# Moving the attention steps of batches 1 and 2 to other places in batch 0 of an attention and bilinear-layer kernel

## The chip, the cores and the metric

The kernel runs on one NeuronCore of a Trainium2 chip. A core has five engines that each work through their own instruction list in order: TensorE (PE; its weight loads are shown as PEld), VectorE (DVE), ScalarE (ACT), GpSimd (POOL, unused here) and SyncE (SP, which issues most of the DMAs). [...] The metric is the device time of one execution in microseconds (us). The kernel before the change took 482.41 us (median of three runs, 482.38 to 482.61).

## The reference

Attention between 512 tokens and 32 states in each of 8 batches and 8 heads, in both directions, then a bilinear layer with two more matrix products:

```python
def _attn_ref(x, state):                       # x (8, 8, 512, 64), state (8, 8, 32, 64)
    scores = scale * np.matmul(x, state.transpose(0, 1, 3, 2))
    a = softmax(scores)                        # over the 32 states
    xread = np.matmul(a, state)
    scores2 = scale * np.matmul(state, x.transpose(0, 1, 3, 2))
    a2 = softmax(scores2)                      # over the 512 tokens
    sread = np.matmul(a2, x)
    return np.concatenate([xread, sread], axis=2)

def _moe_ref(x, w1, w2, w3, w_out):            # x: 8 * 544 rows of 512; w1, w2 (512, 1024)
    a = x @ w1
    b = x @ w2
    h = a * b @ w3
    return (h @ w_out).astype(np.float32)
```

## The kernel before

**The algebra.** Since `xread` is `a @ state`, the kernel multiplies the states by the weights first (`sw`, "state times weights") and the softmax by the result afterwards. `w3 @ w_out` is formed once (`w34`). The softmax over states, transposed, is `at`; the one over tokens is `a2`. Operands of the large products are split into two float32r parts, `hi` and `lo`, by a cast on ACT and a subtraction on DVE (`split`, L100 to L104), and each product is the sum of three.

**The prologue.** The weights arrive as the bits of float64 numbers. `to_f32` (L107) makes float32 of a chunk of 128x1024: ACT turns the high words into a float (`w_sb<-raw` or `w<-raw`, L123) and takes the low words' share (`ulps<-raw`, L131; on DVE, L127, for the first chunks), and after a `yield` DVE shifts (L135) and adds (L139). `raw` has three buffers and `ulps` two. Eight chunks of w1 and w2 go to eight places of `w_sb`: chunks 0 to 3 serve columns 0 to 511 of both (`convert_half(0..3)`), chunks 4 to 7 the other half. `w34` (L629) makes rows of the product in fp32. In the prologue ACT and DVE run in the order in which the code is written, the `go(...)` calls; PE and SP do so in the whole program (`manual_schedule`). Behind `order.close()` the framework's scheduler sets the order on ACT and DVE, by priorities and the `issue_after` hints.

**Batch 0.** `stage1` (L357) is called for eight blocks `ft` of 128 hidden columns: 24 products into a tile of two PSUM banks, then `hidden`: ACT copies one bank (L326), DVE multiplies by the other (L327), `split` makes `g_hi` and `g_lo`. `stage2` and `early_stage2` (L371) project them in pieces of 12 products. Between them stand the small products: a **unit** (`sw_steps`, eight instructions at L152 on 64x32 sub-arrays, recorded as 16) makes one tile of `sw`, the **scores** of a batch are such a unit too, and the **read** (L268, 32 instructions recorded as 64, on 128x32 sub-arrays) makes `sread`. A row of them between products on the full 128x128 array is called a block here. Scores, units, `stage1` sums and reads take their PSUM tile in turn from a pool of three two-bank tiles (`two_banks()`, `ps`): each waits until the engine that reads the third one back has done so.

**Batches 1 to 7** (`quarter_batch`) make the 512x512 product from seven quarter products; the combinations of `w34` for them are made in batch 0 by `combine_weights(k)`, k = 0 to 3 (DVE L413 to L420, an ACT cast, a DVE subtraction; all four go through one buffer `g_x`). Each batch's read and units and the scores of the batch after next form one block.

**A batch's attention steps** (`attention_steps`): the generator `scores` makes the scores, two softmaxes (DVE L200 to L244, ACT L213 and L224), transposes both (`token_order` L229, then 16 small DMAs on SP's queue, `move_blocks` L177; `at` L249) and splits `at`. The `yield`s let the caller spread it. `read_state` multiplies a2 by the tokens (`x_s`, one buffer), scales the result on DVE (`scaled`, L273) and frees its PSUM tile by that.

Of the kernel before, what the change touches and what calls it, by code (L numbers as in the profile page):

```python
# [29 lines left out]
P = 128  # L30
NF = 512
NW = 1024
# [7 lines left out]
def attn_bilinear_kernel(  # L40
# [66 lines left out]
    def to_f32(pool, src, out, ends=(NW,), loads=(), wout=None):  # L107

        raw = pool.tile([P, NW], mybir.dt.int64, name="raw", bufs=3)
        ulps = pool.tile([P, NW], I32, name="ulps", bufs=2)
        parts = [slice(*ends) for ends in zip((0, *ends), ends)]
        for start, stop in zip((0, *loads), (*loads, NW)):
            nc.sync.dma_start(out=raw[:, start:stop], in_=src[:, start:stop])
        for part in parts:  # L120
            words = raw[:, part].bitcast(I32).rearrange("p (n k) -> p k n", k=2)
            high, low = words[:, 1], words[:, 0]
            nc.scalar.activation(  # L123
                out=out[:, part], in_=high.bitcast(F32), func=AF.Prelu, scale=2.0**-112, alpha=-(2.0**32)
            )
            if len(parts) > 1:
                nc.vector.tensor_scalar(  # L127
                    out=ulps[:, part], in0=low.bitcast(U32), scalar1=2.0**-29, scalar2=None, op0=ALU.mult
                )
            else:  # L130
                nc.scalar.activation(out=ulps[:, part], in_=low.bitcast(U32), func=AF.Copy, scale=2.0**-29)  # L131
        yield
        for part in parts:
            bits = out[:, part].bitcast(I32)
            nc.vector.tensor_scalar(out=bits, in0=bits, scalar1=3, scalar2=None, op0=ALU.logical_shift_left)  # L135
            for dest, start, stop in ((wout, 0, DO), (out, DO, NW)) if wout is not None else ((out, 0, NW),):
                piece = slice(max(start, part.start), min(stop, part.stop))
                if piece.start < piece.stop:
                    nc.vector.tensor_tensor(  # L139
                        out=dest[:, piece].bitcast(I32), in0=out[:, piece].bitcast(I32), in1=ulps[:, piece], op=ALU.add  # L140
                    )
# [30 lines left out]

    def move_blocks(dest, src):
# [7 lines left out]
    def attention_steps(b):  # L181
# [3 lines left out]
        def scores():  # L185
# [10 lines left out]
            s1 = work_tile()  # L196
# [8 lines left out]
            nc.vector.transpose(out=flat(s1), in_=flat(ps))  # L205
            if b <= PLAIN:
                token_maxima()
# [19 lines left out]
            def token_order():  # L227
                blocks = work_tile()
                nc.vector.transpose(out=flat(blocks), in_=flat(e2))  # L229
                a2["t"] = work_tile() if b < PLAIN else att.tile([P, KT, S], F32, name="e2", bufs=1)  # L230
# [4 lines left out]
            if b > PLAIN:  # L235
                token_order()
                yield
# [5 lines left out]
            nc.vector.reciprocal(out=sum1, in_=sum1)  # L243
            nc.vector.tensor_tensor(  # L244
# [5 lines left out]
            if b > PLAIN:  # L250
                yield
            at_tiles[b] = [att.tile([P, KT, S], F32R, name=f"at_{part}", bufs=1) for part in ("hi", "lo")]
            last = split(*at_tiles[b], at)
            if b <= PLAIN:
                yield
                with tc.issue_after(last[1].ins):
                    token_order()
# [60 lines left out]
    last_split, stored, last_unit = [], [], []  # L318
# [4 lines left out]
    def hidden(ps, n, g_hi, g_lo):  # L323
        a_sb = main.tile([P, NF], F32, name="tmp", bufs=4)
        with tc.high_priority():
            nc.scalar.copy(out=a_sb[:, :n], in_=ps[:, 0, :n])  # L326
            nc.vector.tensor_tensor(out=a_sb[:, :n], in0=a_sb[:, :n], in1=ps[:, 1, :n], op=ALU.mult)  # L327
# [60 lines left out]
    reads = {}  # L388

    def side_steps():  # L390

        scores, reads[1], _ = attention_steps(1)
        w = sw_steps(1)
        softmax = scores()

        def rest():

            with tc.issue_after(stored[0].ins):
# [73 lines left out]
    def quarter_batch(b):  # L472
# [33 lines left out]
        def next_scores(b):  # L506

            if b < B:
                scores, reads[b], _ = attention_steps(b)
                softmaxes[b] = scores()  # L510
                next(softmaxes[b])

        raw = whole_tile(main, F32)
        stage1_pair(b, 0, raw)
        if b == PLAIN:
            next_scores(b + 1)
            load_x(b + 2)
            first_moves = reads[b](own_banks)
            next(first_moves)
            next(softmaxes[b + 1])  # L520
        softmax = softmaxes.get(b + 1, iter(()))
        next(softmax, None)
        if b == PLAIN:
            next(first_moves, None)
# [5 lines left out]
        if b > PLAIN:  # L530
            next(softmax, None)
# [9 lines left out]
        if b == PLAIN:  # L541
            with behind(took):
                next(softmax)
# [89 lines left out]
    def convert_half(n):  # L633

        return to_f32(pro, w12[n], places[n])
# [38 lines left out]
    go(w2_0), go(w3_6), go(softmax), go(w3_6)  # L674
    w34(5)
    go(softmax)
    go(w2_0)
# [3 lines left out]
    load_tokens(0)  # L681
# [5 lines left out]
    w34(7, range(LAST, FT))  # L687
    finish(7)
    order.close()
    for quarter in range(QT):  # L690
        stage1(0, 2 * quarter, gs)
        if quarter == 1:
            run(sw_steps(0)[2:])
        if quarter:
            early_stage2(quarter - 1)
        if quarter == 1:
            side = side_steps()
        elif quarter == 2:
            run(side.pop(0))
# [124 lines left out]
    softmaxes = {}  # L824
# [48 lines left out]
```

## Time and profile before

| | us |
|---|---|
| median of the runs | 482.41 |
| the profiled execution | 482.62 |
| its span, first to last instruction | 480.8 |
| PE busy | 473.8 |
| DVE busy | 407.7 |
| ACT busy | 239.5 |

The profiled execution's time holds 1.8 us around the span. A row of the timeline gives the start (us from the span's start), how long the merged instructions took, the engine, the line, the operation, the tiles written and read, their shape and count, and in brackets how long the engine had been idle and what ended it. A matmul's row shows its modelled end, so rows of PE overlap: what matters is the distance between starts. A row of the windows gives each engine's busy time in a stretch, the granted TensorE clock and the DMA engines' share.

### The profile page before, as it was taken

What the parts mean: (1) busy time and instruction counts of PE and PEld (TensorE: products, weight loads), DVE (VectorE), ACT (ScalarE), POOL (GpSimd) and SP (SyncE); (2) the same over time, 40 slices, a digit from 0 to 9 for tenths busy, and PEclk for the clock granted to TensorE, in tenths of its full rate; (3) what the DMA queues carried; (4) which work ended last, traced back from release to release, by engine and by line L of the source; (5) the groups of instructions that cost most, each with busy time, mean ns of one, the idle gap of its engine ahead of it and who ended that gap; (6) DMA issues with size and microseconds to landing.
All of it is one profiled execution on the core that took longest, in us unless ns stands there. A gap on an engine that the chain in (4) does not pass through costs nothing.

```text
span 480.8 us, 7935 instructions
## 1 busy us (share of the span) xinstructions
PE 473.8 (99%) x3174; PEld 358.1 (74%) x3174; DVE 407.7 (85%) x511; ACT 239.5 (50%) x306; POOL 0.2 (0%) x4
## 2 busy tenths in 40 slices
PE   7999999999999999999999999999999999999996
PEld 5444457777788688878877887888688868888885
DVE  5669898899789997999699969987998796569987
ACT  4777785464444633643463446254624470335652
POOL 0000000000000000000000000000000000000000
PEclk9999999999999999999999999999999999999999
DMA  8996891432531522052215112421321102001101
GB/s 339 365 365 252 341 354 27 116 110 67 193 77 34 181 70 42 25 207 60 35 46 191 49 30 87 157 57 25 110 70 25 19 26 75 1 0 45 45 1 44
DMA packets 55716, 52.42 MB, mean 109 GB/s; under 512 B 41856, under 2 KB 50560, under 8 KB 51072
## 3 DMA queue, kind: packets, MB, share of 16 engines
q1 hardware_dynamic: 46752, 43.34, 27.7%
q10 hardware_dynamic: 8928, 8.59, 5.1%
q8 instruction: 25, 0.41, 0.4%
q14 instruction: 11, 0.09, 0.1%
HBM read 38.27 MB, written 8.91 MB: 98 GB/s over the span
## 4 chain that ended last, share of the span: by engine, by line
PE 86%; DVE 5%; DMA 5%; ACT 2%; issue 1%; SPq 0%; DVEq 0%; ACTq 0%
PE ps L439 32%; PE ps L466 16%; PE ps_a L466 12%; PE ps L152 6%; PE ps_o L371 5%; PE ps L357 5%; DMA raw<-in_w_k_dram 3%; PE ps L754 3%; PE ps_o L629 3%; PE ps L755 2%; DMA raw<-in_w3t_dram 2%; PE ps L268 2%; PE ps_a L152 1%; DVE tmp L450 1%; ACT ulps L131 1%
## 5 line engine op out<-in xcount | busy, mean ns | idle before, releaser
L439 PE MATMUL ps<-at_lo,sw_hi 128*128 128x512 f32 x224 | 87.4, 390 | 0.0
L439 PE MATMUL ps<-at_hi,sw_hi 128*128 128x512 f32 x224 | 87.3, 390 | 0.0
L439 PE MATMUL ps<-at_hi,sw_lo 128*128 128x512 f32 x224 | 87.3, 390 | 0.0
L102 ACT CAST g_hi<-g_x 128x1024 fp32r<-128x1024 f32 (+2 forms) x61 | 56.7, 939 | 55.2 <-DVE g_x L447 42.3
L103 DVE TENSOR_TENSOR g_lo<-g_x,g_hi 128x1024 fp32r<-128x1024 f32 (+2 forms) x61 | 65.3, 1080 | 9.5 <-ACT g_hi L102 9.4
L445 ACT COPY g_x<-ps 128x1024 f32<-128x1024 f32 x28 | 28.3, 1012 | 73.1 <-PE ps L439 45.2
L447 DVE TENSOR_TENSOR g_x<-g_x,ps 128x1024 f32<-128x1024 f32 x28 | 34.0, 1215 | 29.2 <-PE ps L439 29.2
L439 PEld LDWEIGHTS ps<-at_hi,sw_lo 128*128 128x128 f32 x224 | 42.1, 188 | 8.8
L439 PEld LDWEIGHTS ps<-at_lo,sw_hi 128*128 128x128 f32 x224 | 42.1, 188 | 8.7
L439 PEld LDWEIGHTS ps<-at_hi,sw_hi 128*128 128x128 f32 x224 | 42.1, 188 | 8.4
L466 PE MATMUL ps<-t,g_hi 128*128 128x512 f32 x180 | 45.3, 393 | 0.0
L450 DVE TENSOR_TENSOR g_x<-g_x 128x1024 f32<-128x1024 f32 (+1 forms) x32 | 36.9, 1154 | 0.4
L466 PEld LDWEIGHTS ps<-t,g_hi 128*128 128x128 f32 x180 | 32.3, 189 | 5.6
L450 DVE TENSOR_TENSOR tmp<-tmp,ps 128x512 f32<-128x512 f32 (+1 forms) x48 | 31.3, 651 | 2.0
L103 DVE TENSOR_TENSOR sw_lo<-ps,sw_hi 128x1024 fp32r<-128x1024 f32 (+1 forms) x28 | 30.6, 1138 | 0.2 <-ACT sw_hi L102 0.2
L466 PE MATMUL ps_a<-wo,g_hi 128*128 128x512 f32 x120 | 29.8, 390 | 0.0
L629 PE MATMUL ps_o<-w_sb,w 128*128 128x512 f32 x64 | 28.5, 599 | 0.5 <-DVE w L139 0.5
L466 PEld LDWEIGHTS ps_a<-wo,g_hi 128*128 128x128 f32 x120 | 22.5, 188 | 4.6
L466 PE MATMUL ps<-t,g_lo 128*128 128x256 f32 x180 | 25.6, 284 | 0.0
L102 ACT CAST sw_hi<-ps 128x1024 fp32r<-128x1024 f32 (+1 forms) x28 | 25.2, 973 | 0.6 <-PE ps L152 0.5
L152 PE MATMUL ps<-w_sb,st 64*32 64x512 f32 (+1 forms) x448 | 24.7, 561 | 0.0
L123 ACT ACTIVATE w_sb<-raw 128x1024 f32<-128x1024 f32 (+3 forms) x18 | 18.8, 1057 | 11.8 <-DMA raw<-in_w_k_dram 9.6
(116 smaller groups left out, 776.4 us busy)
## 6 DMA issues: line engine op xcount, KB each, us to landing
raw<-in_w_k_dram SPq DMA_DIRECT2D x8, 1024.0 KB, 6.9
x_d<-in_x_d_dram SPq DMA_DIRECT2D x8, 1024.0 KB, 5.2
raw<-in_w_dram SPq DMA_DIRECT2D x8, 1024.0 KB, 6.9
x_s<-in_x_s_dram SPq DMA_DIRECT2D x8, 1024.0 KB, 5.2
out_dram<-tmp ACTq DMA_DIRECT2D x56, 128.0 KB, 1.8
raw<-in_w3t_dram SPq DMA_DIRECT2D x4, 1024.0 KB, 7.6
e<-work SPq DMA_DIRECT2D x112, 32.0 KB, 1.9
out_dram<-tmp ACTq DMA_DIRECT2D x4, 256.0 KB, 2.0
```

The costliest lines, as they stand in the source:

```text
L102: nc.scalar.copy(out=hi, in_=src),
L103: nc.vector.tensor_tensor(out=lo, in0=src, in1=hi.bitcast(F32), op=ALU.subtract),
L123: nc.scalar.activation(out=out[:, part], in_=high.bitcast(F32), func=AF.Prelu, scale=2.0**-112, alpha=-(2.0**32))
L152: nc.tensor.matmul(ps[j * NS:(j + 1) * NS, q], sts[b][rows, j], moving(rows, j), start=True, stop=True)
L357: nc.tensor.matmul(ps[:, i], w[:, kt, c:c + P], a[:, kt], start=(k == 0), stop=(k == 3 * KT - 1))
L371: nc.tensor.matmul(by_halves(ps[:, :DO]), g, wo[w][:, ft], start=(ft == 0 and k == 0), stop=(ft == FT - 1 and k == 2))
L439: nc.tensor.matmul(ps[:, kk], w[:, kt, cols], a[:, kt], start=(k == 0), stop=(k == 3 * KT - 1))
L445: nc.scalar.copy(out=mine, in_=ps)
L447: return nc.vector.tensor_tensor(out=mine, in0=mine, in1=ps, op=ALU.mult)
L450: return nc.vector.tensor_tensor(out=out, in0=x, in1=y, op=op)
L466: nc.tensor.matmul(ps[:, tt, 1] if n else ps[:, tt], part, weights[:, 0] if n else weights, start=(fresh and k == 0 and n == parts[0]), st ...
L629: nc.tensor.matmul(w34_ps[i][:, :DO], w3s[i][:, k * P:(k + 1) * P], w_out[k], start=(k == 0), stop=(k == FT - 1))
```

## The change

The steps are the same; several are called elsewhere:

- `w3_6`'s second half (shift and add on DVE) is called one step of the softmax earlier: `scores` has one more `yield` ahead of the multiplication by the reciprocal (batch 0 only), and the calls in the prologue follow.
- Chunk 4 of w1/w2 is loaded into the tokens' buffer `x_s` in the prologue (`load_half(QT)`), where the tokens of batch 0 were loaded; those come behind `load_x(1)` now. Chunk 7's low words are taken on DVE instead of ACT.
- `token_order` of batch 0 (a transposition on DVE, then 16 DMAs) is called in the prologue, by way of the yields.
- The scores of batch 1 are called right behind units 2 and 3 of batch 0, in one block with them. Their transposed copy lies in `sread`, which is not yet written then. `token_order` of batch 1 comes ahead of the sums.
- The read of batch 1 and the scores of batch 2 join units 2 and 3 of batch 1; they were called in `quarter_batch(1)` behind its first pair of sums.
- `combine_weights(0)` is started a quarter later, and its two steps hang on other instructions.

```diff
-    def to_f32(pool, src, out, ends=(NW,), loads=(), wout=None):
+    def to_f32(pool, src, out, ends=(NW,), loads=(), wout=None, raw=None, on_vector=False):
-        raw = pool.tile([P, NW], mybir.dt.int64, name="raw", bufs=3)
+        if raw is None:
+            raw = pool.tile([P, NW], mybir.dt.int64, name="raw", bufs=3)
+            for start, stop in zip((0, *loads), (*loads, NW)):
+                nc.sync.dma_start(out=raw[:, start:stop], in_=src[:, start:stop])
...
-            if len(parts) > 1:
+            if len(parts) > 1 or on_vector:
                 nc.vector.tensor_scalar(
                     out=ulps[:, part], in0=low.bitcast(U32), scalar1=2.0**-29, scalar2=None, op0=ALU.mult
                 )
...
-            s1 = work_tile()
+            s1 = as_work(sread) if b == PLAIN else work_tile()
...
             yield
-            if b > PLAIN:
-                token_order()
+            if b >= PLAIN:
+                yield from token_order()
                 yield
...
+            if b < PLAIN:
+                yield
             nc.vector.tensor_tensor(
                 out=s1v, in0=s1v, in1=sum1.unsqueeze(2).broadcast_to([P, J, NS]), op=ALU.mult
             )
...
+        def second_read():
+            second = reads[1]()
+            next(second)
+            run(w[2:])
+            next_scores(2)
+            load_x(3)
+            yield from second
+
         first_read = reads[0]()
-        moves = lambda: first_read
         return [
-            [partial(islice, softmax, 3), partial(load_x, 2)], [partial(islice, first_read, 1), w[0], w[1]], [], [rest, moves],
-            [w[2], w[3]], [],
+            [partial(islice, first_read, 1), w[0], w[1]],
+            [], [rest, lambda: first_read], [second_read], [lambda: islice(softmaxes[2], 1)],
         ]
...
     def convert_half(n):
-        return to_f32(pro, w12[n], places[n])
+        return to_f32(pro, w12[n], places[n], raw=halves_ahead.get(n), on_vector=n == 2 * QT - 1)
+    def load_half(n):
+        place = att.tile([P, NT, H, D], F32, name="x_s", bufs=1)
+        halves_ahead[n] = place.rearrange("p t h d -> p (t h d)").bitcast(mybir.dt.int64)
+        nc.sync.dma_start(out=halves_ahead[n], in_=w12[n])
...
-    go(w2_0), go(w3_6), go(softmax), go(w3_6)
+    go(w2_0), go(w3_6), go(softmax), go(w3_6), go(softmax)
     w34(5)
-    go(softmax)
-    go(w2_0)
+    go(softmax), go(w2_0), go(softmax)
...
-    load_tokens(0)
+    load_half(QT)
...
         if quarter == 1:
             run(sw_steps(0)[2:])
+            next_scores(1)
+            load_x(2)
+            side = side_steps()
...
         if quarter == 0:
             run([partial(convert_half, n) for n in range(4, 2 * QT)])
             load_x(1)
-            with tc.issue_after(last_split[1].ins):
-                go(softmax)
+            load_tokens(0)
+            go(softmax)
...
-        elif quarter == 1:
-            first_sums = combine_weights(0)
-            with tc.issue_after(last_unit[1].ins):
-                go(first_sums)
+        elif quarter < 3:
+            with tc.issue_after(last_mult[0].ins):
+                go(softmaxes[1])
+            if quarter == 2:
+                first_sums = combine_weights(0)
+        else:
             with tc.issue_after(last_split[1].ins):
                 go(first_sums)
```

What this does to the engines' lists, at the three places of which the prediction speaks:

**ACT, the conversion of chunks 4 to 7, before.** `sw_hi` are the casts of the first units, `wo` that of `w34`; the two passes of a chunk are `ulps` and `w_sb`.

```order
L102 CAST sw_hi<-ps_346 128x2x256
L102 CAST sw_hi<-ps_359 128x2x256
L102 CAST wo<-ps_o 128x2x256
L131 ACTIVATE ulps<-raw 128x1024
L123 ACTIVATE w_sb<-raw 128x1024 x2
```

The same place after the change:

```order
L102 CAST sw_hi<-ps_346 128x2x256
L132 ACTIVATE ulps<-x_s 128x1024
L102 CAST sw_hi<-ps_359 128x2x256
L102 CAST wo<-ps_o 128x2x256
L132 ACTIVATE ulps<-raw 128x1024
L124 ACTIVATE w_sb<-x_s 128x1024
L124 ACTIVATE w_sb<-raw 128x1024
```

Chunk 4 is read from `x_s`, and chunk 5's `ulps` pass stands ahead of chunk 4's `w_sb` pass.

**DVE, from chunk 6 to the first three multiplications of `hidden` (L327, in the change L337), before.** The three read the PSUM tiles of the first three `stage1` sums: 406, 426 and 500.

```order
L103 TENSOR_TENSOR wo<-ps_o,wo 128x2x256
L135 TENSOR_SCALAR w_sb<-w_sb 128x1024
L139 ISA w_sb<-w_sb,ulps 128x2048
L327 TENSOR_TENSOR tmp<-tmp,ps_406 128x512
L327 TENSOR_TENSOR tmp<-tmp,ps_426 128x512
L103 TENSOR_TENSOR g_lo<-tmp,g_hi 128x512 x2
L229 STREAM_TRANSPOSE work<-e_261 128x1024
L327 TENSOR_TENSOR tmp<-tmp,ps_500 128x512
```

After the change, where the same sums lie in 408, 428 and 500:

```order
L103 TENSOR_TENSOR wo<-ps_o,wo 128x2x256
L136 TENSOR_SCALAR w_sb<-w_sb 128x1024
L128 TENSOR_SCALAR ulps<-raw 128x1024
L140 ISA w_sb<-w_sb,ulps 128x2048
L337 TENSOR_TENSOR tmp<-tmp,ps_408 128x512
L136 TENSOR_SCALAR w_sb<-w_sb 128x1024
L140 ISA w_sb<-w_sb,ulps 128x2048
L337 TENSOR_TENSOR tmp<-tmp,ps_428 128x512
L103 TENSOR_TENSOR g_lo<-tmp,g_hi 128x512 x2
L337 TENSOR_TENSOR tmp<-tmp,ps_500 128x512
```

Chunk 6 now stands ahead of the first multiplication and chunk 7 between the first and the second; one `ulps` pass is new on DVE; the transposition of `e` went ahead of all rows shown.

**PE, the block of units 2 and 3 of batch 1, after the change** (before, its rows 2 and 3 alone stood here):

```order
L277 MATMUL ps_866<-x_s,e_637 32x64 x32
L153 MATMUL ps_904<-w_sb,st 32x512 x8
L153 MATMUL ps_917<-w_sb,st 32x512 x8
L153 MATMUL ps_930<-x_d,st 32x512 x8
L382 MATMUL ps_o<-wo,g_hi 128x512 x2
```

The scores of batch 2 (930) are the third tile behind the read (866) and take its PSUM tile, which `scaled` frees. On DVE these rows lead up to it:

```order
L103 TENSOR_TENSOR sw_lo<-ps_787,sw_hi 128x1024
L103 TENSOR_TENSOR t<-g_x,t 128x4x256
L437 TENSOR_TENSOR g_x<-wo 128x4x256
L442 TENSOR_TENSOR g_x<-g_x 128x2x256
L103 TENSOR_TENSOR at_lo<-work,at_hi 128x1024
L443 TENSOR_TENSOR g_x<-g_x 128x256
L444 TENSOR_TENSOR g_x<-g_x 128x256
L103 TENSOR_TENSOR t<-g_x,t 128x4x256
L437 TENSOR_TENSOR g_x<-wo 128x4x256
L282 TENSOR_TENSOR scaled<-ps_866,sum_596 128x128
```

All of combination 1 (the first row `g_x<-wo` to the second `t<-g_x,t`) and the first addition of combination 2 stand ahead of `scaled`.

More of the change, by code (lines that the diff above doesn't have):

```diff
@@ L243, in scores @@
             nc.vector.reciprocal(out=sum1, in_=sum1)
+            if b < PLAIN:
+                yield
             nc.vector.tensor_tensor(
@@ L249, in scores @@
             nc.vector.transpose(out=flat(at), in_=flat(s1))
-            if b > PLAIN:
+            if b != PLAIN:
                 yield
             at_tiles[b] = [att.tile([P, KT, S], F32R, name=f"at_{part}", bufs=1) for part in ("hi", "lo")]
-            last = split(*at_tiles[b], at)
-            if b <= PLAIN:
+            split(*at_tiles[b], at)
+            if b < PLAIN:
                 yield
-                with tc.issue_after(last[1].ins):
-                    token_order()
+                yield from token_order()
         def read_state(place=two_banks):
@@ L386, in store, with next_scores @@
             queue.dma_start(out=dest, in_=o[first:first + n])
-    reads = {}
+    reads, softmaxes = {}, {}
+    def next_scores(b):
+        if b < B:
+            scores, reads[b], _ = attention_steps(b)
+            softmaxes[b] = scores()
+            next(softmaxes[b])
     def side_steps():
-        scores, reads[1], _ = attention_steps(1)
         w = sw_steps(1)
-        softmax = scores()
+        softmax = softmaxes[1]
         def rest():
-            with tc.issue_after(stored[0].ins):
+            with tc.issue_after(stored[0].ins), tc.issue_after(last_mult[0].ins):
                 yield from softmax
+        def second_read():
[5 more added lines that the diff above has]
+            yield from second
         first_read = reads[0]()
-        moves = lambda: first_read
         return [
-            [partial(islice, softmax, 3), partial(load_x, 2)], [partial(islice, first_read, 1), w[0], w[1]], [], [rest, moves],
-            [w[2], w[3]], [],
+            [partial(islice, first_read, 1), w[0], w[1]],
+            [], [rest, lambda: first_read], [second_read], [lambda: islice(softmaxes[2], 1)],
         ]
@@ L529, in quarter_batch @@
         s3 = quarter(raw[:, :, first])
-        if b > PLAIN:
-            next(softmax, None)
+        next(softmax, None)
         x = whole_tile(late, F32)
@@ L540, in quarter_batch @@
         took = take(m1, bank_a)
-        if b == PLAIN:
-            with behind(took):
-                next(softmax)
         with behind(took):
@@ L696, in attn_bilinear_kernel @@
         if quarter == 1:
-            side = side_steps()
+            go(softmaxes[1])
         elif quarter == 2:
-            run(side.pop(0))
+            with tc.issue_after(last_split[1].ins):
+                go(softmaxes[1])
+        elif quarter == 3:
+            with tc.issue_after(last_mult[0].ins):
+                go(first_sums)
         stage1(0, 2 * quarter + 1, gs)
@@ L703, in attn_bilinear_kernel @@
             load_x(1)
-            with tc.issue_after(last_split[1].ins):
-                go(softmax)
+            load_tokens(0)
+            go(softmax)
             pro_pool.close()
@@ L708, in attn_bilinear_kernel @@
             t_both = late.tile([P, 4, QF, 2, HO], F32R, name="t")
-        elif quarter == 1:
-            first_sums = combine_weights(0)
-            with tc.issue_after(last_unit[1].ins):
-                go(first_sums)
+        elif quarter < 3:
+            with tc.issue_after(last_mult[0].ins):
+                go(softmaxes[1])
+            if quarter == 2:
+                first_sums = combine_weights(0)
+        else:
             with tc.issue_after(last_split[1].ins):
@@ L821, in state_rows @@
         stored(m1, 0, 1)
-    softmaxes = {}
     for b in range(PLAIN, B):
```

26 lines of the change are left out of this document (9 added, 17 removed).

## The prediction

> **What bounds the kernel now.** I read the page's busy times and DMA issues first, then four stretches (busy time of PE, PEld, DVE, ACT and POOL with counts, the granted clock, the DMA share and GB/s), then PE's timeline for the distances between starts.
>
> ```profile
> PE 473.8 (99%) x3174; PEld 358.1 (74%) x3174; DVE 407.7 (85%) x511; ACT 239.5 (50%) x306; POOL 0.2 (0%) x4
> x_s<-in_x_s_dram SPq DMA_DIRECT2D x8, 1024.0 KB, 5.2
> 0.00:10.00 10.00, 7.47 (x35) 6.14 (x36) 4.42 (x12) 3.81 (x5) 0.20 (x4) 1.00 0.80 320
> 51.00:68.00 17.00, 16.74 (x99) 7.41 (x100) 15.27 (x19) 14.55 (x17) 0.00 (x0) 1.00 0.95 349
> 98.00:120.00 22.00, 22.00 (x204) 15.64 (x202) 21.54 (x27) 10.46 (x15) 0.00 (x0) 1.00 0.31 97
> 467.00:481.00 14.00, 9.82 (x56) 8.32 (x54) 9.88 (x21) 4.02 (x9) 0.00 (x0) 0.93 0.13 38
> ```
>
> PE sets the time: it is busy in all of 98 to 120 and nearly all of 51 to 68. So a microsecond less between its starts is one less at the end, and a wait on PE is never made good. But DVE is at 98% in 98 to 120 and at 90% in 51 to 68, the two stretches into which the change moves work. PE's timeline shows what can be won:
>
> ```profile
> 7.88 2.05 PE L616 MATMUL ps_o<-w_sb 128*128 128x512 f32 x4 [1.49 <-DVE w_sb L139]
> 36.80 14.00 PE L629 MATMUL ps_o<-w_sb,w 128*128 128x512 f32 x32
> 51.26 7.11 PE L629 MATMUL ps_o<-w_sb,w 128*128 128x512 f32 x16 [0.46 <-DVE w L139]
> 75.78 1.95 PE L152 MATMUL ps<-w_sb,st 64*32 64x512 f32 x32
> 88.44 0.39 PE L371 MATMUL ps_o<-wo,g_lo 128*128 128x512 f32 x1
> 88.76 1.09 PE L152 MATMUL ps<-x_d,st 64*32 64x512 f32 x16
> 90.11 0.39 PE L357 MATMUL ps<-at_hi,sw_hi 128*128 128x512 f32 x1
> 101.03 1.10 PE L268 MATMUL ps<-x_s,work 128*32 128x64 f32 x64
> 103.94 3.02 PE L371 MATMUL ps_o<-wo,g_x 128*128 128x512 f32 x12
> 112.32 1.95 PE L152 MATMUL ps<-w_sb,st 64*32 64x512 f32 x32
> 155.03 1.10 PE L268 MATMUL ps<-x_s,e 128*32 128x64 f32 x64
> 157.80 2.78 PE L152 MATMUL ps<-w_sb,st 64*32 64x512 f32 x48
> ```
>
> **The gains.** First, two blocks less. The scores of batch 1 stand alone at 88.76. Between the last L371 before them and the second L357 behind them lie 90.11 - 88.44 = 1.67 us; two full-array products take 0.23 each (36 take the 8.38 from 103.94 to 112.32), so the block costs 1.21. In a block with others a unit adds 1.95 - 1.09 = 0.86. Joining saves 0.35, and so does the second merging (read 1 and scores 2 into the block at 112.32, their own block going): **0.70 us**. Second, the wait of 0.46 at 51.26: L629 steps by 0.43 (14.00 less a 0.60 tail over 31 steps), so its next start was due at 50.63 and came 0.63 late, behind w3_6's add on DVE.
>
> ```profile
> 49.89 1.23 DVE L139 CUSTOM_DVE_ANT_0 w<-w,ulps 128x2048 uint16<-128x2048 uint16 x1
> 51.03 1.24 DVE L249 STREAM_TRANSPOSE work<-work 128x1024 f32<-128x1024 f32 x1
> 53.38 1.23 DVE L103 TENSOR_TENSOR at_lo<-work,at_hi 128x1024 fp32r<-128x1024 f32 x1 [1.11 <-ACT at_hi L102]
> 62.88 1.28 DVE L103 TENSOR_TENSOR sw_lo<-ps,sw_hi 128x512 fp32r<-128x512 f32 x2
> 64.67 0.68 DVE L135 TENSOR_SCALAR w_sb<-w_sb 128x1024 int32<-128x1024 int32 x1
> 74.22 1.28 DVE L327 TENSOR_TENSOR tmp<-tmp,ps 128x512 f32<-128x512 f32 x2
> 76.80 1.24 DVE L229 STREAM_TRANSPOSE work<-e 128x1024 f32<-128x1024 f32 x1
> 77.96 0.65 DVE L327 TENSOR_TENSOR tmp<-tmp,ps 128x512 f32<-128x512 f32 x1
> L127 DVE TENSOR_SCALAR ulps<-raw 128x512 int32<-128x512 uint32 x2 | 0.8, 420 | 0.0
> 47.89 1.18 ACT L131 ACTIVATE ulps<-raw 128x1024 int32<-128x1024 uint32 x1
> 52.30 1.04 ACT L102 CAST at_hi<-work 128x1024 fp32r<-128x1024 f32 x1 [3.23 <-DVE work L249]
> 61.54 1.20 ACT L131 ACTIVATE ulps<-raw 128x1024 int32<-128x1024 uint32 x1
> 62.61 1.18 ACT L123 ACTIVATE w_sb<-raw 128x1024 f32<-128x1024 f32 x1
> 78.64 0.62 ACT L102 CAST g_hi<-tmp 128x512 fp32r<-128x512 f32 x1 [2.01 <-DVE tmp L327]
> ```
>
> With the softmax's multiplication behind it, the add can begin when ACT's ulps pass ends, 49.07, and ends at 50.4, before 50.63. **0.62 us** gone. Together -1.32.
>
> **The first new wait: units 2 and 3 of batch 0.** Before, PE came to unit 3 at 75.78 + 0.93 = 76.71, and its PSUM tile was free: the second multiplication of `hidden` had ended at 74.22 + 1.28 = 75.50. Now PE comes at 76.71 - 0.62 = 76.1. What DVE has to do by then:
>
> - The multiplication and the transposition follow the add, which holds DVE for 1.14 (51.03 - 49.89): 49.15 + 1.14 + 1.26 + 1.24 = 52.8, so ACT's `at_hi` comes at 52.87 instead of 52.30. From there ACT has no gap up to chunk 4's `w_sb` pass: 62.61 - 52.30 = 10.31, and one more ulps pass (chunk 5's, 1.07) stands ahead of it. It begins at 64.25 and ends at 65.4.
> - DVE would be there at 64.1: the 1.11 ahead of `at_lo` are filled with chunk 1's shift and add, of which the new wait for the ulps takes half back. It waits 1.4 us at an instruction behind which all of DVE's list is queued, and starts chunk 4's shift at 65.5, not 64.67.
> - From that shift to the end of the second multiplication it was 75.50 - 64.67 = 10.83. The transposition of `e` (a step of 77.96 - 76.80 = 1.16) and chunk 7's ulps now come within it, and about 0.5 goes where an add that stood behind its own shift gets other work in between. The ulps pass on DVE isn't shown at this size; 0.42 for 512 elements and 0.68 for the shift of 1024 say 0.7, a step of 0.61 (1.23 if it ran at the rate of a two-input row). 65.5 + 10.83 + 1.16 + 0.61 - 0.5 = **77.6**.
>
> PE waits 77.6 - 76.1 = **1.5 us** at unit 3. Then the scores of batch 1, joined here, need the third multiplication: ACT's cast (0.1 + 0.50), its copy (about as long), the multiplication (0.1 + 0.68) put it at 79.6; PE is ready at 77.7 + 0.86 = 78.5: **1.1 us** more. Before, this multiplication ended at 77.96 + 0.65 = 78.6 and the scores stood ten microseconds behind it. Bounds: 1.1 if ACT were in time, 3.1 with the slow ulps pass. I take 2.6, since ACT's gapless list leaves no slack.
>
> **The second new wait: the scores of batch 2.** Now the tile needed is that of read 1, two units earlier, and `scaled` on DVE frees it.
>
> ```profile
> 101.81 0.69 DVE L327 TENSOR_TENSOR tmp<-tmp,ps 128x512 f32<-128x512 f32 x1 [0.17 <-ACT tmp L326]
> 112.83 1.18 DVE L413 TENSOR_TENSOR g_x<-wo 128x1024 f32<-128x1024 f32 x1
> 128.68 0.28 DVE L273 TENSOR_TENSOR scaled<-ps_a,sum 128x128 f32<-128x128 f32 x1
> L418 DVE TENSOR_TENSOR g_x<-g_x 128x512 f32<-128x512 f32 x4 | 2.7, 686 | 0.1
> L419 DVE TENSOR_TENSOR g_x<-g_x 128x256 f32<-128x256 f32 x4 | 1.7, 422 | 0.1
> L103 DVE TENSOR_TENSOR t<-g_x,t 128x1024 fp32r<-128x1024 f32 x4 | 4.9, 1226 | 1.4 <-ACT t L102 1.4
> 109.44 1.05 ACT L102 CAST t<-g_x 128x1024 fp32r<-128x1024 f32 x1 [0.92 <-DVE g_x L420]
> 112.97 11.51 SPq L177 DMA_DIRECT2D e<-work x16
> ```
>
> Count from R, the start of read 0 (101.03 before). PE reaches the scores of batch 2 at R + 2.91 (to 103.94) + 8.38 (to 112.32) + 2.77 (a read and two units, 155.03 to 157.80) = R + 14.1. DVE's last multiplication of `hidden` starts at R + 0.78, and combination 2's addition came 11.02 later. In between the transposition of `e` is gone (-1.16), and all of combination 0 but its first addition has come in: 0.60 + 0.34 + 0.34 + 1.14 plus 0.3 between dependent rows = 2.7. Combination 1's last subtraction now ends with nothing left to do before ACT's cast of `t` (1.05 and two semaphores): 1.2. The addition itself takes 1.2 (combination 2 reuses the buffer that the subtraction before it reads) and `scaled` 0.3: R + 0.78 + 11.02 - 1.16 + 2.7 + 1.2 + 1.2 + 0.3 = R + 16.1. PE waits **2.1 us**. Bounds: 0.9 if the cast is hidden, 2.6 with more gaps. Before, `scaled` came at 128.68 in its turn among other rows, and nobody was waiting for it.
>
> **What I cost at nothing.** The 16 DMAs of batch 1 now hold SP's queue for 11.5 us from about 94, by the same counting; the tokens of batch 1, queued behind them, are issued at 106 and land 5 us later, and read 1 comes at R + 11.3, with R = 101.03 - 0.62 + 2.6 - 0.35 = 102.7 that is 114. Three microseconds of cover; without it the delay is PE's. Batch 0's tokens, now behind batch 1's `x_d`, and its 16 DMAs have some 30 us until read 0. Chunk 4's load is as large as the one that it displaces and lands before ACT comes to it.
>
> **Sum.** 482.62 - 1.32 + 2.6 + 2.1 = 486.0 for an execution like the profiled one; that lies 0.21 above the median, so **485.8 us**, 0.7% slower.
>
> **Rivals.** *No waits* (the other side): DVE and ACT fill their gaps and both tiles are free in time; the time is 482.41 - 1.32 = 481.1 us. It takes DVE 1.5 us earlier at 76 and 2.1 at R + 14; for it speaks that before neither tile was late, against it the gapless ACT row and 98% of DVE. It decides as soon as all waits together are under 1.3 us: 0.07. *Waits about as large as the gain* (both at their lower bounds, 1.1 + 0.9): 483.1, within the noise or just above: 0.05. *One wait only*, because DVE is less late in one of the places than its rows say: 483.2 without the first, hardly to be told from no change (0.06), 483.7 without the second (0.09). *More waits*: the third and fourth sums of batch 1 need tiles which ACT and DVE free behind a backlog of the batch 2 softmax, with a margin of half a microsecond by the same counting, so perhaps 1 us more: 486.8; or the granted clock falls after a pause of 2 us, as in the tail (0.93 over 14 us, that is 1 us lost): 486.8. Against the clock: PE stood 1.49 us ahead of its first L616 within the first 10 us, at 1.00. Together 0.10. The forecast itself: 0.63.
>
> [...]
>
> The forecast's own range is 485.0 to 486.6; 8 in 10 reach from 483.3 to 487.0. A measurement of this kernel can tell about 0.2% (1 us) from no change: faster 0.07, same 0.05 + 0.06 = 0.11, slower 0.82.
>
> **What would show it.** Right: no idle time ahead of the third `w34` product; PE idle 1 to 2 us at unit 3 and about 1 at the scores of batch 1, both put down to DVE's multiplication; 2 us at the scores of batch 2, put down to `scaled`; DVE idle over 1 us for ACT's chunk 4; all stages behind it as long as before. Wrong: units 2 and 3 and the scores in one stretch of 2.8 us, or `scaled` within 1.7 us of its read.

## The result, and where the time went

The changed kernel took 485.39 us, median of six executions (485.33 to 487.67), beside 482.58 for the kernel before on the same chip: a ratio of 1.0065 over all executions, 95% interval 1.0051 to 1.0079 (the two medians alone give 1.0058). It is 2.8 us slower.

Four of the six executions lie between 485.33 and 485.41. In the other two, the profiled one among them (487.67, span 485.9), the granted clock fell for a while, which is told below; the profiled one also began its first `w34` product 0.48 us late (37.28, not 36.80). So the waits are read here as distances between neighbouring starts.

The page's busy times of the engines after the change:

```profile
PE 475.5 (98%) x3174; PEld 359.0 (74%) x3174; DVE 407.5 (84%) x512; ACT 238.3 (49%) x305; POOL 0.2 (0%) x4
```

PE is idle for 485.9 - 475.5 = 10.4 us, before it was 480.8 - 473.8 = 7.0: 3.4 us more of waiting. The 1.7 us more of busy time for the same products are the slower clock of this execution.

PE's timeline after the change: units 2 and 3 and the scores of batch 1; then the projection and its piece for token tile 2; then the read of batch 1, two units and the scores of batch 2.

```profile
75.57 1.09 PE L153 MATMUL ps<-w_sb,st 64*32 64x512 f32 x16
77.83 1.09 PE L153 MATMUL ps<-w_sb,st 64*32 64x512 f32 x16 [1.17 <-DVE tmp L337]
79.81 1.61 PE L153 MATMUL ps<-x_d,st 64*32 64x512 f32 x16 [0.88 <-DVE tmp L337]
...
107.31 3.02 PE L382 MATMUL ps_o<-wo,g_x 128*128 128x512 f32 x12
112.01 0.72 PE L382 MATMUL ps_o<-wo,g_hi 128*128 128x512 f32 x2 [1.68 <-ACT tmp L395]
...
117.69 1.10 PE L277 MATMUL ps<-x_s,e 128*32 128x64 f32 x64
118.72 1.95 PE L153 MATMUL ps<-w_sb,st 64*32 64x512 f32 x32
120.50 1.09 PE L153 MATMUL ps<-x_d,st 64*32 64x512 f32 x16
```

Three waits are new. Unit 3 starts 1.37 us later than its regular step of 0.89 behind unit 2, and the scores of batch 1 another 1.09, both put down to DVE's multiplication of `hidden`, as forecast. The third is where I had none: 1.84 us ahead of token tile 2, put down to a copy on ACT. At the scores of batch 2, where I had forecast 2.1, it is 0.03. With the gain as predicted, -1.32 + 1.37 + 1.09 + 1.84 + 0.03 = +3.0; measured were +2.81. The wait at unit 3 differs between executions: where the lists up to there are the same, two other runs below show 1.11 and 1.06, and with these the sum is +2.7.

DVE and then ACT at the first two waits:

```profile
65.77 0.69 DVE L136 TENSOR_SCALAR w_sb<-w_sb 128x1024 int32<-128x1024 int32 x1 [1.29 <-ACT w_sb L124]
...
72.91 0.68 DVE L128 TENSOR_SCALAR ulps<-raw 128x1024 int32<-128x1024 uint32 x1
...
74.64 0.68 DVE L337 TENSOR_TENSOR tmp<-tmp,ps 128x512 f32<-128x512 f32 x1
...
77.10 0.68 DVE L337 TENSOR_TENSOR tmp<-tmp,ps 128x512 f32<-128x512 f32 x1
77.69 1.46 DVE L103 TENSOR_TENSOR g_lo<-tmp,g_hi 128x512 fp32r<-128x512 f32 x2
79.07 0.68 DVE L337 TENSOR_TENSOR tmp<-tmp,ps 128x512 f32<-128x512 f32 x1
```

```profile
75.35 0.62 ACT L102 CAST g_hi<-tmp 128x512 fp32r<-128x512 f32 x1 [2.88 <-DVE tmp L337]
75.87 0.58 ACT L335 COPY tmp<-ps 128x512 f32<-128x512 f32 x1
77.81 0.62 ACT L102 CAST g_hi<-tmp 128x512 fp32r<-128x512 f32 x1 [1.35 <-DVE tmp L337]
78.34 0.58 ACT L335 COPY tmp<-ps 128x512 f32<-128x512 f32 x1
```

DVE waits 1.29 us for ACT's pass over chunk 4 and ends the second multiplication at 77.78, that is 77.30 without the late start, where the forecast said 77.6 (in the two other runs it ends at 77.04 and 76.98). One thing differs from the kernel before, where ACT took both copies first and then both casts:

```profile
72.88 1.04 ACT L326 COPY tmp<-ps 128x512 f32<-128x512 f32 x2
74.94 1.22 ACT L102 CAST g_hi<-tmp 128x512 fp32r<-128x512 f32 x2 [1.02 <-DVE tmp L327]
```

Now each copy stands behind the cast of the product before it, and that cast waits for a DVE multiplication. ACT and DVE at the third wait:

```profile
110.42 1.04 ACT L102 CAST t<-g_x 128x1024 fp32r<-128x1024 f32 x1 [1.86 <-DVE g_x L444]
111.38 0.58 ACT L395 COPY tmp<-ps_o 128x512 f32<-128x512 f32 x1
```

```profile
109.98 0.41 DVE L444 TENSOR_TENSOR g_x<-g_x 128x256 f32<-128x256 f32 x1
...
117.76 1.23 DVE L103 TENSOR_TENSOR t<-g_x,t 128x1024 fp32r<-128x1024 f32 x1 [1.11 <-ACT t L102]
119.02 1.22 DVE L437 TENSOR_TENSOR g_x<-wo 128x1024 f32<-128x1024 f32 x1
120.16 0.28 DVE L282 TENSOR_TENSOR scaled<-ps,sum 128x128 f32<-128x128 f32 x1
```

The copy at 111.38 frees the projection's PSUM tile of token tile 0, which token tile 2 takes again (`ps_o`, two buffers). In ACT's list it stands behind the cast of combination 0's `t`, and that waits for combination 0's last subtraction on DVE. `scaled` ends at 120.44, that is R + 16.04 (R = 104.40, the start of read 0); PE was by then held up by 1.84 and came to the scores just as it ended.

The clock: three stretches of 3.42, 3.42 and 1.60 us, with busy times of PE, PEld, DVE, ACT and POOL and then the granted clock.

```profile
76.83:80.25 3.42, 1.53 (x24) 0.37 (x32) 2.84 (x5) 1.57 (x3) 0.00 (x0) 1.00 0.29 48
80.25:83.67 3.42, 3.42 (x22) 1.84 (x7) 3.01 (x4) 1.98 (x3) 0.00 (x0) 0.50 0.30 49
83.67:85.27 1.60, 1.60 (x9) 1.31 (x7) 1.19 (x2) 0.00 (x0) 0.00 (x0) 1.00 0.82 205
```

Right behind the two waits the clock is halved for 3.42 us; the scores and the projection's first pieces take some 1.6 us longer.

### The profile page after: what moved, and what is told of

The parts are those of the page before. It is cut to its first block, busy times and chain, and to the rows that moved or that the text cites. A ratio compares the mean times of both kernels' runs of the same rounds, so it can differ in the third digit from the quotient of the medians.

```text
span 485.9 us, 7922 instructions
## 1 busy us (share of the span) xinstructions
PE 475.5 (98%) x3174; PEld 359.0 (74%) x3174; DVE 407.5 (84%) x512; ACT 238.3 (49%) x305; POOL 0.2 (0%) x4
## 4 chain that ended last, share of the span: by engine, by line
PE 79%; DVE 8%; DMA 5%; ACT 5%; issue 1%; ACTq 0%; DVEq 0%
PE ps L463 31%; PE ps L490 16%; PE ps_a L490 12%; PE ps L153 5%; PE ps_o L382 4%; DMA raw<-in_w_k_dram 4%; PE ps L776 3%; PE ps L368 3%; ACT ulps L132 2%; DMA raw<-in_w3t_dram 2%; PE ps L777 2%; PE ps L277 1%; ACT w_sb L124 1%; PE ps_a L153 1%; DVE tmp L474 1%
## 5 line engine op out<-in xcount | busy, mean ns | idle before, releaser
L634 PEld LDWEIGHTS ps_o<-w_sb,w 128*128 128x128 f32 x64 | 11.9, 190 | 15.9 <-issue 14.0
```

Source lines behind the costliest of these rows:

```text
L634: nc.tensor.matmul(w34_ps[i][:, :DO], w3s[i][:, k * P:(k + 1) * P], w_out[k], start=(k == 0), stop=(k == FT - 1))
```

## The experiments

All edits start from the changed kernel unless it is said. The table gives the median, the ratio to the kernel before (95% interval), the four waits on PE in us (start later than the regular step), and in how many executions the mean granted clock was 0.996 or less.

| run | us | ratio | unit 3 | scores 1 | token tile 2 | scores 2 | clock low |
|---|---|---|---|---|---|---|---|
| the change | 485.39 | 1.0065 (1.0051 to 1.0079) | 1.37 | 1.09 | 1.84 | 0.03 | 2 of 6 |
| store first | 484.15 | 1.0028 (1.0017 to 1.0039) | 1.11 | 1.08 | 0 | 0.77 | 1 of 7 |
| combination early | 485.86 | 1.0070 (1.0056 to 1.0083) | 1.06 | 1.08 | 0 | 0 | 4 of 6 |
| relief, before the third | 487.80 | 1.0094 (1.0078 to 1.0110) | 0.82 | 2.21 | 1.84 | 0.05 | 3 of 5 |
| relief, behind the third | 485.20 | 1.0049 (1.0037 to 1.0061) | 0.92 | 1.08 | 1.84 | 0.05 | 0 of 5 |
| copies first | 485.40 | 1.0057 (1.0045 to 1.0069) | 1.02 | 1.08 | 1.85 | 0.05 | 1 of 6 |
| copies first and relief | 483.86 | 1.0020 (1.0012 to 1.0029) | 0 | 0.83 | 1.85 | 0.03 | 0 of 11 |
| all three places | 481.83 | 0.9982 (0.9973 to 0.9991) | 0 | 0.58 | 0 | 0 | 0 of 11 |
| scores 1 apart | 488.13 | 1.0109 (1.0096 to 1.0123) | 1.35 | - | 1.70 | 0 | 2 of 4 |
| third copy too | 481.63 | 0.9978 (0.9969 to 0.9987) | 0 | 0 | 0 | 0 | 0 of 11 |
| add first alone, in the kernel before | 483.25 | 1.0009 (1.0000 to 1.0018) | 0 | - | 0 | - | 0 of 11 |

Each wait is that of one profiled execution. In the change, store first, combination early and scores 1 apart the lists up to unit 3 are the same, and its wait lies between 1.06 and 1.37; so differences of 0.3 in that column say nothing by themselves.

### The wait at token tile 2: the store's copy first

```diff
         combine(out=t[:, 3], in0=raw[:, 2], in1=t[:, 1])
+        yield
         split(t_both[:, :, k, 0], t_both[:, :, k, 1], t)
...
         run(side[tt])
+        if tt == 0:
+            with tc.issue_after(stored[0].ins):
+                go(first_sums)
```

> The edit: combination 0's cast of t and its remainder are put behind the copy that stores the projection tile of token tile 0 in ACT's list; by the same edit DVE gets scaled of read 1 one addition (1.2 us) earlier. Theory A (the wait of 1.84 us at token tile 2 is ACT's list: the copy that frees the PSUM tile stands behind a cast that waits for DVE's last subtraction): this wait goes to zero, and the one that I had forecast comes out behind it. PE then reaches the scores of batch 2 at R + 14.2 (R: the start of read 0), scaled ends at R + 16.0 - 1.2 = R + 14.9, or R + 15.5 if the later cast holds DVE by 0.6: a wait of 0.7 to 1.3 us, put down to scaled. Time 485.4 - 1.84 + 0.7 to 1.3 = 484.2 to 484.9. Theory B (PE waits at token tile 2 for something else, or the store's copy is late for its own reason): the wait stays at 1.5 us or more at token tile 2, no wait at the scores of batch 2, time 485.2 to 485.6.

PE and DVE of this run:

```profile
116.03 1.95 PE L153 MATMUL ps<-w_sb,st 64*32 64x512 f32 x32
118.55 1.09 PE L153 MATMUL ps<-x_d,st 64*32 64x512 f32 x16 [0.57 <-DVE scaled L282]
```

```profile
118.21 0.28 DVE L282 TENSOR_TENSOR scaled<-ps,sum 128x128 f32<-128x128 f32 x1
118.41 1.22 DVE L437 TENSOR_TENSOR g_x<-wo 128x1024 f32<-128x1024 f32 x1
```

Theory A holds in place and size: the 1.84 are gone, and the wait that I had forecast comes out behind them, 0.77 us, put down to `scaled`. Both came from one backlog on DVE; PE met the earlier of the two tiles first.

### The same wait: combination 0 early

```diff
             side = side_steps()
+            first_sums = combine_weights(0)
+            with tc.issue_after(last_unit[1].ins):
+                go(first_sums)
+                go(first_sums)
...
-        elif quarter == 3:
-            with tc.issue_after(last_mult[0].ins):
-                go(first_sums)
```

(The other call of `go(first_sums)`, at the end of the quarters, is gone too.)

> The edit: the whole combination 0 is done right behind units 2 and 3 of batch 0, where DVE stands idle for 3.95 us, and no longer ahead of the projection. Theory A (combination 0's five DVE instructions and its cast on ACT are what makes both the tile of token tile 2 and scaled late): neither wait is left, scaled ends at about R + 16.0 - 3.9 = R + 12.1 while PE is at R + 14.2; time 485.4 - 1.87 = 483.5, up to 484.0 if the 4.9 us of the combination (its cast included) reach past the idle time and make the next multiplication late. Theory B (DVE's total load behind read 0 is the cause, whatever is in it): at least half of the wait stays at one of the two places, time 484.5 to 485.4.

Both waits went, as theory A has it, but the time did not. PE at the second projection:

```profile
90.40 0.73 PE L382 MATMUL ps_o<-wo,g_hi 128*128 128x512 f32 x2 [1.19 <-ACT g_hi L102]
91.48 0.50 PE L382 MATMUL ps_o<-wo,g_lo 128*128 128x512 f32 x1 [0.35 <-DVE g_lo L103]
```

The combination with its cast takes 4.9 us, and the multiplication behind it is late for the projection. From the second projection to the third PE takes 98.68 - 88.37 = 10.31 us, in the run with the copies first (below) 96.44 - 88.28 = 8.16: 2.15 us come back there for 1.87 saved. The undisturbed executions are at 485.4 to 485.5, 1.5 us above what I expected. The idle stretch of 3.95 us on DVE, on which I had counted, was read in the execution with the halved clock, which puts PE off by 1.6 us just there. At the full clock, with the copies first, it is 2.36:

```profile
86.39 0.69 DVE L338 TENSOR_TENSOR tmp<-tmp,ps 128x512 f32<-128x512 f32 x1 [2.36 <-ACT tmp L336]
```

### The first two waits: relief for DVE

In the first run chunk 7's low words are taken on ACT again and batch 0's transposition of `e` stands behind the second split; in the second run it stands behind the third multiplication. The diff is that of the first; in the second both calls stand behind `stage1(0, 2)`, the first of them with `issue_after(last_mult[0].ins)`.

```diff
-        return to_f32(pro, w12[n], places[n], raw=halves_ahead.get(n), on_vector=n == 2 * QT - 1)
+        return to_f32(pro, w12[n], places[n], raw=halves_ahead.get(n))
...
     w34(7, range(LAST, FT))
-    go(softmax)
     finish(7)
...
             load_tokens(0)
+            with tc.issue_after(last_split[1].ins):
+                go(softmax)
             go(softmax)
```

> The edit: chunk 7's ulps pass is back on ACT, and the transposition of e of batch 0 stands behind the second hidden multiplication's split again, but ahead of the third multiplication. Theory A (unit 3 and the scores of batch 1 wait for the second and the third multiplication, and only what stands ahead of the third sets their sum): 1.77 us of work leave the list ahead of the second multiplication, so unit 3 waits 0 to 0.2 us instead of 1.37; the transposition and the split stand ahead of the third, so the scores wait about 2.2 instead of 1.09, the sum stays near 2.3; time 485.2 to 485.5. Theory B (as my prediction adds it: each microsecond put ahead on DVE is one more of waiting, so taking 1.77 away takes 1.77 off the sum): the waits come to 0.7 together, time 483.6 to 483.8.

> The edit: as in the run before this one, but the transposition of e stands behind the third multiplication. Theory A: unit 3 waits 0 to 0.2; the third multiplication cannot begin before the second split's cast and the copy that stand in turn on ACT, so it ends some 1.9 us after the second, and the scores of batch 1 still wait about 1.1 us; sum 1.2 against 2.46 measured; time 484.0 to 484.4. Theory B (DVE's list alone sets it, and it is empty in time): both waits gone, time 482.9 to 483.1. In both the wait of 1.84 at token tile 2 stays. If the granted clock falls because of the two waits next to each other, executions with 2 us more (2 of 6 before) should not be seen here.

Both were worse than expected by theory A and far from theory B (the first took 486.3 in the executions with the full clock). With 1.8 us of work taken off DVE's list, unit 3 still waited 0.8 to 0.9 us. DVE and ACT of the second run:

```profile
74.25 0.68 DVE L337 TENSOR_TENSOR tmp<-tmp,ps 128x512 f32<-128x512 f32 x1
75.62 0.69 DVE L103 TENSOR_TENSOR g_lo<-tmp,g_hi 128x512 fp32r<-128x512 f32 x1 [0.68 <-ACT g_hi L102]
76.23 0.68 DVE L337 TENSOR_TENSOR tmp<-tmp,ps 128x512 f32<-128x512 f32 x1
77.59 0.69 DVE L103 TENSOR_TENSOR g_lo<-tmp,g_hi 128x512 fp32r<-128x512 f32 x1 [0.69 <-ACT g_hi L102]
78.20 0.68 DVE L337 TENSOR_TENSOR tmp<-tmp,ps 128x512 f32<-128x512 f32 x1
```

```profile
74.97 0.62 ACT L102 CAST g_hi<-tmp 128x512 fp32r<-128x512 f32 x1 [2.13 <-DVE tmp L337]
75.49 0.58 ACT L335 COPY tmp<-ps 128x512 f32<-128x512 f32 x1
```

DVE has nothing more to do and is idle between the multiplications. They are 1.98 us apart: a multiplication, the cast that waits for it, the copy behind the cast, and only then the next multiplication. So DVE's list was not the only limit. That gave theory C.

### Two limits, one behind the other: copies first

ACT's cast and DVE's remainder of the first hidden product are held back until the copy of the second has been issued; in the first run that is the only edit, in the second the relief (behind the third) is there too. `holding` is set during `stage1(0, 0)` alone.

```diff
-            nc.scalar.copy(out=a_sb[:, :n], in_=ps[:, 0, :n])
+            copied = nc.scalar.copy(out=a_sb[:, :n], in_=ps[:, 0, :n])
...
-            last_split[:] = split(g_hi, g_lo, a_sb[:, :n])
+            held.append(partial(split, g_hi, g_lo, a_sb[:, :n]))
+            if not holding:
+                with tc.issue_after(copied.ins):
+                    for step in held:
+                        last_split[:] = step()
+                held.clear()
```

> The edit: only ACT's list changes: the copy of the second hidden product out of PSUM stands ahead of the cast of the first (before the change it stood so, after it the cast came first); DVE's list stays as after the change. Theory C (two limits lie one behind the other: the chain multiplication, cast, copy, multiplication over ACT, 1.98 us a step, and DVE's list with the transposition, the ulps and the last chunk): taking away the chain alone changes nothing, since DVE's list holds the second multiplication to the same time and has both remainders ahead of the third; unit 3 still waits 1.0 to 1.2, the scores of batch 1 0.9 to 1.1; time 485.2 to 485.5. Theory D (the chain over ACT alone sets both): both waits fall by about 0.9, time 483.5 to 484.

> The edit: ACT's copies ahead of the cast as in the run before this one, and DVE relieved as in the earlier run (chunk 7's ulps on ACT, the transposition of e behind the third multiplication), which alone came to 485.2. Theory C (both limits have to go): the first two multiplications come back to back at about 74.3 and 74.9, PE comes to unit 3 at 76.1 and does not wait; the third ends near 77.5 and PE is ready at 77.0: a wait of 0 to 0.5. Sum 0 to 0.5 against 2.0; time 483.2 to 483.7, with the wait of 1.84 at token tile 2 unchanged. Rival: a third limit holds PE there (the DVE load behind it, or the input of the scores): the sum stays above 1.2, time 484.4 or more.

Either edit alone does next to nothing (485.40 and 485.20), both together take 1.5 us off (483.86). Theory C holds. DVE, ACT and PE with both:

```profile
74.48 1.28 DVE L338 TENSOR_TENSOR tmp<-tmp,ps 128x512 f32<-128x512 f32 x2
```

```profile
72.44 1.10 ACT L336 COPY tmp<-ps 128x512 f32<-128x512 f32 x2
```

```profile
75.22 1.95 PE L153 MATMUL ps<-w_sb,st 64*32 64x512 f32 x32
77.79 1.09 PE L153 MATMUL ps<-x_d,st 64*32 64x512 f32 x16 [0.62 <-DVE tmp L338]
```

Units 2 and 3 run in one stretch again. The scores wait 0.83, more than the 0 to 0.5 expected, and the time is 0.2 above the range.

### All three places, and the third copy too

To the last kernel comes a split placement of combination 0: its four additions and subtractions in DVE's idle stretch behind units 2 and 3, its cast and remainder behind the store's copy, as in the first two experiments. In the second run the second split is held as well, until the third copy has been issued.

> The edit: the run before this one, and of combination 0 the four additions and subtractions put into DVE's idle time behind units 2 and 3 of batch 0, its cast and remainder left behind the store's copy of token tile 0. Theory (the three places are all that the change costs, and each has its cause as found): no wait of more than 0.5 us on PE from the start of the hidden products to the scores of batch 2; scaled ends before R + 14.2. The gain of 1.32 is then left whole: 482.6 - 1.32 + 0 to 0.5 = 481.3 to 481.8, faster than before the change. Rival (the combination's new place makes the next multiplication late, as when all of it stood there, 1.35 + 0.35 us at the second projection): 482.8 to 483.4.

> The edit: the run with all three places mended, and on ACT the copy of the third hidden product now also stands ahead of the second cast, so that on DVE the third multiplication stands ahead of the second remainder. Theory (the 0.58 us still waited at the scores of batch 1 are this step of the chain over ACT): the third multiplication ends 0.6 us earlier, the wait falls to 0.1 or less, time 481.8 - 0.5 = 481.2 to 481.4. Rival (the copy is held by its PSUM tile, which PE fills only at the end of the hidden products): the wait stays above 0.3, time 481.5 to 481.8.

```profile
74.98 1.95 PE L153 MATMUL ps<-w_sb,st 64*32 64x512 f32 x32
77.30 1.09 PE L153 MATMUL ps<-x_d,st 64*32 64x512 f32 x16 [0.38 <-DVE tmp L338]
```

481.83, at the upper edge of what was expected: with all of its waits gone but 0.58 us, the change is 0.18% faster than the kernel before instead of 0.65% slower. The third copy takes the last 0.58 us at the scores away, but PE then comes to the second projection at 86.22 and not at 86.64, while DVE's remainder for it still ends at 87.5, and 0.35 are waited there. So the theory was right about the wait at the scores and 0.2 too low in the time; 481.63 is below both kernels (0.22% faster than before).

### Scores 1 apart

The scores of batch 1 are called behind the second projection again, in quarter 2 and not in quarter 1.

```diff
-            next_scores(1)
-            load_x(2)
-            side = side_steps()
...
+        if quarter == 2:
+            next_scores(1)
+            load_x(2)
+            side = side_steps()
+            go(softmaxes[1])
```

> The edit: the scores of batch 1 stand alone again, behind the second projection, as before the change; all else as after it. If the wait at the scores is the price of joining them: unit 3 still waits 1.1, the wait of 1.09 goes, a block of its own costs 0.35 again, and 1.84 stays at token tile 2: 485.4 - 1.09 + 0.35 = 484.6. If the later start of batch 1's softmax pushes its rows into the stretch behind read 0, the waits there grow by up to a microsecond: 485.0 to 485.6. If the granted clock falls because of the two waits next to each other, no execution here should be 2 us longer than the rest.

A miss: 488.13. Two of its four executions have the full clock, and they too take 487.3 and 487.7. SP's queue and PE:

```profile
100.01 11.73 SPq L181 DMA_DIRECT2D e<-work  x16
111.85 8.35 SPq L165 DMA_DIRECT2D x_s<-in_x_s_dram  x2
```

```profile
117.37 2.48 PE L277 MATMUL ps<-x_s,e 128*32 128x64 f32 x64 [2.49 <-DMA out_dram<-tmp]
```

Batch 1's 16 small DMAs begin 1.7 us ahead of read 0 (100.01 against 101.67), in the changed kernel 8.4 (95.98 against 104.40). The tokens of batch 1 are issued behind them at 111.85, and 5.3 us (the median time to landing of these loads in this run) put them at 117.15. The read starts at 117.37, 2.5 us late. The row names a store's DMA as what came last, but the semaphores in the trace show the tokens: the last completion of their load is recorded at 117.12, and PE's wait for that semaphore ends at 117.15. In this place the clock fell too (0.50 from 117.38 to 120.80).

### One gain alone, in the kernel before

```diff
+            if b < PLAIN:
+                yield
             nc.vector.tensor_tensor(
                 out=s1v, in0=s1v, in1=sum1.unsqueeze(2).broadcast_to([P, J, NS]), op=ALU.mult
             )
...
-    go(w2_0), go(w3_6), go(softmax), go(w3_6)
+    go(w2_0), go(w3_6), go(softmax), go(w3_6), go(softmax)
```

> The edit: the kernel before, with one part of the change alone: the softmax's multiplication put behind the add of w3's seventh chunk. Theory (the gap of 0.63 us at the third w34 product was on the path, and nothing behind it uses up the gain): 482.75 - 0.62 = 482.1 to 482.2, no idle time ahead of that product. Rival (DVE is then 0.6 us later with the transposition, ACT's later rows slip, and the second hidden multiplication takes the gain back, as a wait at unit 3): 482.6 to 482.9.

```profile
53.54 1.23 DVE L103 TENSOR_TENSOR at_lo<-work,at_hi 128x1024 fp32r<-128x1024 f32 x1 [1.11 <-ACT at_hi L102]
...
57.97 1.23 DVE L139 CUSTOM_DVE_ANT_0 w<-w,ulps 128x2048 uint16<-128x2048 uint16 x1
```

```profile
59.34 4.53 PE L631 MATMUL ps_o<-w_sb,w 128*128 128x512 f32 x10 [0.65 <-DVE w L139]
```

The rival won, at another place than it named: the idle time at the third `w34` product is gone, and 0.65 us stand ahead of the fourth, behind the add of w3's last chunk. DVE is still idle 1.11 us ahead of `at_lo`. No gain: 483.25 against 482.71, which is 0.35 above even the rival's range. In the profiled execution 0.33 us more are lost at the third projection, behind DVE's `g_lo`; where the rest goes stays open.

## Why the prediction was right, and where it was not

**Time and range.** 485.8 was forecast, 485.39 measured, inside the range. The sum came out for partly other reasons than it gave.

**The idle time at the third `w34` product (-0.62).** Right in the changed kernel: the hidden products start at 66.4 in the runs whose prologue is not late, 67.11 before. But the last experiment shows that the edit to which I put it down is worth nothing alone. By the changed kernel's rows it counts only with the other calls, by which chunk 1's shift and add fill the 1.11 us ahead of `at_lo`: w3's last add then starts at 57.51 in spite of the late prologue, 57.97 with the yield alone. Both together were not tried in the kernel before. I named that filling, but for another term.

**Two blocks less (-0.35 each).** Right. From the projection to read 2 the kernel with all three places mended takes 153.97 - 103.24 = 50.73 us, before 155.03 - 103.94 = 51.09: 0.36 for the second merging. For the first, from units 2 and 3 to the third projection, the kernel with the third copy takes 94.79 - 75.14 = 19.65, less its 0.35 of waiting, against 95.37 - 75.78 = 19.59: 0.29.

**The first new wait (+2.6).** Place, releasers and size right (1.37 + 1.09), the account of it half wrong. The step that failed is the one that counts DVE's list alone up to the second multiplication and adds the transposition and the `ulps` as 1.16 + 0.61. As steps between starts they measured 1.16 and 0.6 (and PE's step to unit 3 is 0.89, not 0.93), but taking both away bought 0.2 us. Behind DVE's list stood the chain over ACT, 1.98 us a step, because the copy of a product was now behind the cast of the one before. I had used this chain for the third multiplication and not for the second. Its end lies close to that of DVE's list (the second multiplication starts at 76.23 by the chain, in the run with the relief behind the third, and at 76.30 and 76.36 by the list in the runs that kept it), so that a sum over the list alone gave nearly the right size was luck. ACT's late pass over chunk 4 is there as forecast (DVE idle 1.29, forecast 1.4); no run took it away, so its share was not measured apart. Which part of the change turned ACT's order round was not tried either.

**The second new wait (+2.1).** Size nearly right (1.84 + 0.03), place wrong. The backlog was counted right: `scaled` ended at R + 16.04, forecast R + 16.1. (The terms of the forecast add up to R + 16.04 as well, and so to a wait of 2.0, not 2.1.) What the step left out is that the same backlog holds ACT's cast of `t`, behind which stands the copy that frees the projection's PSUM tile; PE needs that tile ten microseconds before the one that I looked at. Moving the copy ahead brought the forecast wait out (0.77 with `scaled` one addition earlier).

**What was costed at nothing.** It cost nothing in the changed kernel. That the tokens' place in SP's queue is a real price with some microseconds of cover shows in the run with the scores apart: the softmax's small DMAs began 6.8 us later against read 0, and the read of batch 1 was 2.5 us late.

**The rivals.** "No waits" at 481.1 needed both tiles in time; with the causes removed the kernel comes to 481.6 to 481.8, so its price was nearly right and its condition was not met. The falling clock was a rival at 0.10 with other mechanisms. It came in two executions of six, which took 1.6 and 2.3 us longer (0.48 of the latter from the prologue), too few to move the median. My argument against it, that PE's pause of 1.49 us in the first 10 us left the clock at 1.00, looked at one pause and not at two close together; the last section gives what was measured ahead of each fall.

## What to carry to other kernels

A stall that two engines explain equally well may have two causes that hide each other: take both away before believing that either is free. When a backlog on one engine grows, list every tile that is freed behind it, on other engines' lists too, and look for the one that is needed first, since it takes the wait from all later ones. A gap that is closed is a gain only when the next thing that the same engine feeds is early as well.

## What was unexpected of the hardware

The granted clock fell to half (0.50) in a stretch in which PE was never idle for more than 1.2 us at a time. Ahead of the fall lay 3.42 us in which PE was busy for 1.53, with small products between two waits. The kernels without waits there, or with up to 0.83 us at one of the two places, never showed it (0 of 11 executions in three of them); with 0.9 to 1.4 and 1.1 it came in 4 of 24 (four kernels; a fifth, with a new pair of waits 10 us later, in 4 of 6), and with 0.8 and 2.2 in 3 of 5. The wait of 1.84 us at token tile 2, between full-array products, did not bring it in 11 executions of the kernel in which it was nearly alone.

Three of the profiled executions have such a fall before the end of the run. In the 3.4 us ahead of it PE was busy for 1.53 us in the changed kernel (45%), for 1.61 in store first (47%) and for 0.92 in scores 1 apart (27%). In two other stretches of this length the clock stayed at 1.00: PE was busy for 1.73 us (51%) about the one wait at token tile 2 with the copies first, and for 1.92 (56%) about the pause of 1.49 us in the prologue (4.72 to 8.13, kernel before). The stretch ahead of the fall in store first, and that with the copies first:

```profile
75.73:79.14 3.41, 1.61 (x35) 0.26 (x31) 3.20 (x5) 1.20 (x3) 0.00 (x0) 1.00 0.32 53
107.19:110.60 3.41, 1.73 (x8) 1.11 (x7) 3.38 (x5) 2.14 (x4) 0.00 (x0) 1.00 0.68 284
```

The amount of waiting alone does not tell the executions apart. In the profiled execution of the relief before the third, with waits of 0.82 and 2.21 us, PE was busy for 1.09 of the 3.41 us from 76.26 on, less than ahead of the fall in the changed kernel, and the mean granted clock of the execution was 1.000; so it was in that of combination early, with 1.06 and 1.08. In three and four other executions of these two kernels it was 0.994 to 0.996. That two waits of about a microsecond close together can bring the fall where one of 1.84 does not is my estimate from these stretches and the counts above; no run was made to test it.
